# A block-causal attention and two-MoE-layer kernel on one core: weights, x and activations moved to multiples of 2048 or 512 bytes of SBUF, with two buffers of exponentials in place of three

## The chip, the cores and the metric

The kernel runs on one core of one Trainium2 chip. The metric is the device time of one execution in microseconds (us). A core has a matrix engine (TensorE, called PE here, with PEld for its loads of the stationary operand), three engines for elementwise work (VectorE or DVE, ScalarE or ACT, GpSimd or POOL), and SP, which issues the DMAs of this kernel. All of them work on SBUF, 128 partitions wide; an address in this text is the byte offset of a tile inside a partition. PE writes its results to eight banks of PSUM.

## What is computed

Batch 4, 8 heads, 576 positions, head size 64; 2304 tokens of 512 values after attention.

```python
scores = scale * q @ k^T, blocks of 64, causal by block; attn = softmax(scores); x = attn @ v   # x: 2304 x 512
h  = x @ w_in                      # 512 -> 1024
e  = exp(h - max(h)); sm = e / (sum(e) + 1e-09)
solu = h * sm
ln = (solu - mean(solu)) / sqrt(var(solu) + 1e-06) * g_ln
x2 = ln @ w_out                    # 1024 -> 512
h2 = x2 @ w2_in                    # 512 -> 2048
out = (h2 * tanh(softplus(h2))) @ w2_out   # Mish, 2048 -> 512
```

## The kernel before

**Precision.** Nearly every fp32 product is made of three products of fp32r halves: an operand is split into a high part (copied to fp32r) and a low part (the rest), and high x high, high x low and low x high are summed in one PSUM bank. So weights and activations lie in SBUF as pairs: `wih`/`wil`, `woh`/`wol` for the first layer, `w2ih`/`w2il`, `w2oh`/`w2ol` for the second, `xh`/`xl`, `lth`/`ltl`, `x2h`/`x2l`, `gh`/`gl` for what flows through.

**Order of the work.** The program first adds every piece of work to a list (`Plan.add`) with its engine, an estimated cost, the keys that it reads and writes, a priority from the table `PRIO`, and the PSUM banks that it takes and frees. `Plan.order` then walks through time and picks, for each engine, the ready piece of lowest priority number; the instructions are issued in that order, and each engine carries out its own in that order. A piece that writes a buffer waits in this plan for the readers of the buffer's last content, so the number of buffers of a `Rot` (a ring of equal tiles) is one of the things that set the order. Waits on the chip come from the same tiles.

**Stages.**
- Attention, 32 heads (`head`, lines 480 to 722): transposes of k and q, scores, exponentials, normalising on POOL, transposes of the probabilities, the product with v into `xt`. All its tiles lie in the pool `at`.
- First layer, 18 tiles of 128 tokens (`moe1_tile`, line 734), put among the heads as soon as a batch's x is there, the last eight and a half behind the attention. Per tile: x is split into `xh`, `xl` (POOL); line 763 makes h, 24 matmuls of 512 columns into two banks; DVE takes the maxima (776), ACT the exponentials into the tile `e` (781), DVE multiplies with h and normalises in `e` (790), ACT sums squares (795), POOL does the power and the normalising of `e` (801, 803), and line 816 transposes `e` in eight pieces. ACT and DVE split the transposed result into `lth` and `ltl` (823, 824).
- Per two tiles, `moe1_x2` makes x2 (line 833): 96 matmuls of 256 columns, with woh or wol as stationary and lth or ltl as moving operand. x2 goes to DRAM.
- Second layer: six groups of 384 tokens, first with the first 1024 hidden values (half A, weights in the right-hand pool `m2a`, opened when the last head is done), then with the others (half B, weights in the left-hand pool `m2b`, opened when the first layer is done). Per group and chunk of 128 hidden values (`moe2_chunk`): 12 matmuls of 384 columns (line 927), Mish (936), the split into `gh`, `gl`, and 9 matmuls of 512 columns (line 945).

The matmuls that this text speaks of:

```python
 763  nc.tensor.matmul(
 764      out=ps(hp[hf]), lhsT=x.t[:, kk, :], rhs=w[:, kk, hf * 512:(hf + 1) * 512],
 833  nc.tensor.matmul(
 834      out=ps(s)[:, (c % 2) * 256:(c % 2) * 256 + 256], lhsT=w[:, kk, cs], rhs=x.t[:, kk, :],
 927  nc.tensor.matmul(out=h(), lhsT=w[wk][:, kk, ms], rhs=x.t[:, kk, :],
 945  nc.tensor.matmul(out=ps(oslots[t]), lhsT=x.t[:, tsl], rhs=w[wk][:, m, :],
```

`lhsT` is the stationary operand, loaded before each matmul; `rhs` is the moving one. The profile writes `ps<-moving,stationary`.

**Where the tiles lie.** A pool places its tiles one behind the other in the order in which they are made. `const` begins at the bottom; on it stand `m1` (left, first layer) and later, in its place, `m2b`. The right-hand pools (`at`, later `m2a`) are laid so that they end at the top. The table under "The change" has the addresses.

The tiles that the change touches: `e_r`, a ring of three tiles of 4096 bytes (line 727), `g_sb` (line 421, 32 bytes, before the rings of raw weights), `st_r` (line 728, four tiles of 32 bytes), and the ends of `const` and `m2a` (`open_right`, line 870).

Of the kernel before, what the change touches and what calls it, by code (L numbers as in the profile page):

```python
# [10 lines left out]
F32 = mybir.dt.float32  # L11
# [189 lines left out]
def kernel(  # L201
# [17 lines left out]
    P = 128  # L219
    KD = DM // P  # L220
    KF = DFF // P
# [39 lines left out]
    const = ctx.enter_context(tc.tile_pool(name="const", bufs=1))  # L261
# [17 lines left out]
    m1 = m1_cm.__enter__()  # L279
# [138 lines left out]
    wil = m1.tile([P, KD, DFF], F32R, name="wil")  # L418
    woh = m1.tile([P, KF, DM], F32R, name="woh")
    wol = m1.tile([P, KF, DM], F32R, name="wol")  # L420
    g_sb = m1.tile([P, KF], F32, name="g_sb")
    raw1 = Rot(m1, "wraw", 2, (P, 512, 2), I32)
    em1 = Rot(m1, "wem", 2, (P, 2, 512), I32)

# [299 lines left out]

    xh_r = Rot(m1, "xh", 2, (P, KD, P), F32R)
    xl_r = Rot(m1, "xl", 2, (P, KD, P), F32R)
    e_r = Rot(m1, "e", 3, (P, 2, 512), F32)
    st_r = Rot(m1, "st", 4, (P, 8), F32)
    jk_r = Rot(m1, "jk", 1, (P, 2, 512), BF16)
    lth_r = Rot(m1, "lth", 1, (P, KF, 2 * P), F32R)  # L730
    ltl_r = Rot(m1, "ltl", 1, (P, KF, 2 * P), F32R)
    xo_r = Rot(const, "xo", 2, (P, 2, 256), F32)

    def moe1_tile(i, xts, lth, ltl):
        xh, xl = xh_r.next(), xl_r.next()
# [134 lines left out]
    def open_right():  # L870
        at_cm.__exit__(None, None, None)
        cm = tc.tile_pool(name="m2a", bufs=1, side="right")
        p = cm.__enter__()
        opened["r"] = cm
        for nm, shape in (("i", [P, KD, NA * P]), ("o", [P, NA, DM])):
            for x in "hl":
                wa_h[nm + x] = p.tile(shape, F32R, name=f"w2{nm}{x}a")
        x2r_r.make(p)
        x2h_r.make(p, 1)
        x2l_r.make(p, 1)  # L880

    def open_left():
        m1_cm.__exit__(None, None, None)
        cm = tc.tile_pool(name="m2b", bufs=1, side="left")
        p = cm.__enter__()
        opened["l"] = cm
        for nm, shape in (("i", [P, KD, NB * P]), ("o", [P, NB, DM])):
            for x in "hl":
                wb_h[nm + x] = p.tile(shape, F32R, name=f"w2{nm}{x}b")
        x2h_r.make(p)  # L890
        x2l_r.make(p)
        for r in (s_r, gh_r, gl_r, ob_r, raw2, em2, ac_r):
            r.make(p)
# [105 lines left out]
    for b in range(B):  # L999
# [5 lines left out]
        while nt < NTILE and (nt + 1) * P <= (b + 1) * S:  # L1005
# [3 lines left out]
            if nt % 2 == 1:  # L1009
                moe1_x2(nt // 2, *lts[nt // 2])  # L1010
            nt += 1
    o = add(HOST, 0.0, open_right, w=[RIGHT], prio=-1000)
    o.deps.update(heads)
    weights2(0, raw1, em1, WP2A, RIGHT)
# [46 lines left out]
```

## Time and profile before

| | |
|---|---|
| three runs | 875.48, 878.86, 877.20 us; median 877.2 |
| the profiled execution | 877.13 us in all, span of its instructions 875.3 us |
| TensorE clock granted, mean over the span | 0.996 |
| busy share: PE, PEld, DVE, ACT, POOL | 97%, 87%, 58%, 59%, 39% |
| DMA | 74.50 MB, mean 85 GB/s |

A busy PE is not PE at its peak: matmuls overlap, and the ends that the profile gives them are modelled, so the mean duration of one (say 337 ns) is longer than the time from one start to the next. The pace is read from the chain of waits instead, where a piece such as "x24" is so many matmuls of one line back to back and its duration is their time from start to start. The profile's 40 slices are about 22 us each.

### The profile page before, as it was taken

The page shows a single profiled execution, that of the slowest core. Times are in us where ns is not written, and L with a number is a line of the kernel's source. Part 1 is how long each engine was busy: PE and PEld are TensorE (multiplying, and loading weights), DVE is VectorE, ACT ScalarE, POOL GpSimd, SP SyncE. Part 2 cuts the span into 40 slices and gives each one's busy share as a digit, 9 for nine tenths or more (in the row PEclk, how much of TensorE's full clock was granted, in tenths as well). Part 3 has the DMA queues.
Part 4 walks back from the last instruction along what each step waited for, and adds up shares of the span by engine and source line. Part 5 has one row for each costly group of instructions (what it writes and reads, how often), then busy time and mean ns, then how long its engine had stood idle before and what let it go on. Part 6 is the DMA issues. An engine that isn't in the chain of part 4 may idle for free.

```text
span 875.3 us, 14647 instructions
## 1 busy us (share of the span) xinstructions
PE 852.8 (97%) x5152; PEld 764.3 (87%) x5152; DVE 509.4 (58%) x1259; ACT 513.6 (59%) x1278; POOL 339.0 (39%) x440
## 2 busy tenths in 40 slices
PE   4999999999999999999999999999999999999998
PEld 4777878778999999999999899988998989999996
DVE  6889898999887885899962646621111122122121
ACT  6999879888787874666653767643333233133231
POOL 5877867779675551533112334212011011011000
PEclk9999989999999999999999999999999999999999
DMA  8554433413523101523322454321022031230120
GB/s 205 116 135 117 97 100 98 107 37 68 122 47 77 40 14 41 162 101 109 106 69 80 133 180 142 100 72 43 31 73 73 1 109 26 82 109 29 46 73 36
DMA packets 108009, 74.50 MB, mean 85 GB/s; under 512 B 84128, under 2 KB 94880, under 8 KB 107936
## 3 DMA queue, kind: packets, MB, share of 16 engines
q1 hardware_dynamic: 107936, 73.57, 29.2%
q8 instruction: 40, 0.66, 0.3%
q14 instruction: 33, 0.27, 0.1%
HBM read 59.40 MB, written 14.16 MB: 84 GB/s over the span
## 4 chain that ended last, share of the span: by engine, by line
PE 85%; DVE 8%; ACT 5%; DMA 1%; issue 1%; POOL 0%; SPq 0%; ACTq 0%; DVEq 0%
PE ps L927 21%; PE ps L945 21%; PE ps L833 11%; PE ps L763 10%; PE ps L566 5%; PE ps L700 5%; PE ps L648 4%; PE ps L673 3%; PE ps L530 2%; PE ps L816 2%; ACT pt L608 1%; DMA wraw<-in_moe_w_in_dram 1%; DVE nmx L589 1%; DVE ptl L256 1%; PE ps L533 1%
## 5 line engine op out<-in xcount | busy, mean ns | idle before, releaser
L256 DVE TENSOR_TENSOR gl<-s,gh 128x384 fp32r<-128x384 f32 x96 | 61.7, 644 | 247.9 <-ACT gh L250 247.9
L936 ACT ACTIVATE s<-ps 128x384 f32<-128x384 f32 x96 | 47.1, 490 | 193.7 <-PE ps L927 193.5
L259 POOL TENSOR_TENSOR x2l<-x2r,x2h 128x384 fp32r<-128x384 f32 x48 | 52.2, 1116 | 239.9 <-ACT x2h L250 221.4
L608 ACT ACTIVATE pt<-ps,nmx 128x288 f32<-128x288 f32 (+2 forms) x192 | 91.5, 491 | 19.8 <-DVE nmx L589 11.8
L631 POOL TENSOR_SCALAR pt<-pt,sm 128x64 f32<-128x64 f32 (+4 forms) x160 | 86.5, 561 | 39.4 <-DVE sm L626 16.6
L833 PE MATMUL ps<-lth,woh 128*128 128x256 f32 x288 | 82.8, 288 | 0.1
L833 PE MATMUL ps<-lth,wol 128*128 128x256 f32 x288 | 80.8, 281 | 0.0
L833 PE MATMUL ps<-ltl,woh 128*128 128x256 f32 x288 | 80.8, 280 | 0.0
L589 DVE TENSOR_REDUCE nmx<-ps 128x1 f32<-128x448 f32 (+3 forms) x192 | 73.9, 419 | 5.5 <-PE ps L566 3.4
L700 PE MATMUL ps<-identr,pt 128*128 128x128 f32 x480 | 69.5, 280 | 2.0 <-DVE xt L658 0.7
L927 PE MATMUL ps<-x2h,w2ilb 128*128 128x384 f32 x192 | 64.7, 337 | 0.0
L927 PE MATMUL ps<-x2h,w2ihb 128*128 128x384 f32 x192 | 64.7, 337 | 0.0
L927 PE MATMUL ps<-x2l,w2ihb 128*128 128x384 f32 x192 | 64.6, 337 | 0.0
L927 PE MATMUL ps<-x2h,w2iha 128*128 128x384 f32 x192 | 64.6, 336 | 0.0
L927 PE MATMUL ps<-x2h,w2ila 128*128 128x384 f32 x192 | 64.6, 336 | 0.0
L927 PE MATMUL ps<-x2l,w2iha 128*128 128x384 f32 x192 | 64.4, 335 | 0.0
L566 PE MATMUL ps<-kth,qt 128*128 128x288 f32 (+2 forms) x192 | 58.2, 315 | 3.1 <-ACT qt L250 1.7
L700 PEld LDWEIGHTS ps<-identr,pt 128*128 128x128 f32 x480 | 54.0, 143 | 4.9 <-ACT ptw L711 1.0
L945 PE MATMUL ps<-w2oha,gl 128*128 128x512 f32 x144 | 57.1, 396 | 0.2 <-DVE gl L256 0.2
L945 PE MATMUL ps<-w2oha,gh 128*128 128x512 f32 x144 | 56.9, 395 | 0.1
L945 PE MATMUL ps<-w2ola,gh 128*128 128x512 f32 x144 | 56.8, 394 | 0.0
L945 PE MATMUL ps<-w2ohb,gl 128*128 128x512 f32 x144 | 56.2, 391 | 0.0
(126 smaller groups left out, 2411.3 us busy)
## 6 DMA issues: line engine op xcount, KB each, us to landing
wraw<-in_moe_w_in_dram SPq DMA_DIRECT2D x24, 512.0 KB, 4.7
wraw<-in_moe_w_out_dram SPq DMA_DIRECT2D x24, 512.0 KB, 3.7
kraw<-in_k_dram SPq DMA_DIRECT2D x60, 160.0 KB, 3.0
x2r<-x_d SPq DMA_DIRECT2D x12, 768.0 KB, 4.8
qraw<-in_q_dram SPq DMA_DIRECT2D x31, 160.0 KB, 2.6
x_d<-xo SPq DMA_DIRECT2D x18, 256.0 KB, 2.3
acc_d<-ob SPq DMA_DIRECT2D x18, 256.0 KB, 2.2
ac<-acc_d SPq DMA_DIRECT2D x18, 256.0 KB, 5.5
```

The lines of the kernel that those rows point to most:

```text
L256: nc.vector.tensor_tensor(out=dst, in0=src, in1=hi.bitcast(F32), op=ALU.subtract)
L259: nc.gpsimd.tensor_tensor(out=dst, in0=src, in1=hi.bitcast(F32), op=ALU.subtract)
L566: nc.tensor.matmul(out=dst, lhsT=qt.t[:, t * P:(t + 1) * P], rhs=m.t[:, c0:c1], start=(i == 0), stop=(i == 1))
L589: nc.vector.tensor_reduce(out=nmx.t[:, j:j + 1], in_=ps(s)[:, o:o + c1 - c0], axis=AX.X, op=ALU.max, negate=True)
L608: add(ACT, c_act(c1 - c0, acc=True), lambda t=t, o=o, c0=c0, c1=c1, j=j: nc.scalar.activation(out=pts[t].t[:, c0:c1], in_=ps(s)[:, o:o + c ...
L631: nc.gpsimd.tensor_scalar(pp, pp, sm.t[:, t:t + 1], 1.0, op0=ALU.mult, op1=ALU.mult)
L700: nc.tensor.transpose(ps(s)[:, i * P:(i + 1) * P], pts[t].t[:, j * P:(j + 1) * P], ident)
L763: nc.tensor.matmul(out=ps(hp[hf]), lhsT=x.t[:, kk, :], rhs=w[:, kk, hf * 512:(hf + 1) * 512], start=bool(first), stop=bool(last))
L833: nc.tensor.matmul(out=ps(s)[:, (c % 2) * 256:(c % 2) * 256 + 256], lhsT=w[:, kk, cs], rhs=x.t[:, kk, :], start=(kk == 0 and i == 0), stop ...
L927: nc.tensor.matmul(out=h(), lhsT=w[wk][:, kk, ms], rhs=x.t[:, kk, :], start=(kk == 0 and i == 0), stop=(kk == KD - 1 and i == 2))
L936: add(ACT, c_act(G2), lambda: nc.scalar.activation(out=s.t, in_=h(), func=AF.Mish), r=[hk, LEFT], w=[s.key()], rel=[hp], prio=pri("f_v" + ...
L945: nc.tensor.matmul(out=ps(oslots[t]), lhsT=x.t[:, tsl], rhs=w[wk][:, m, :], start=(m == 0 and i == 0), stop=(m == n - 1 and i == 2))
```

## The change

It makes no new instruction and takes none away. It does four things to the tiles:
- the ring of exponentials has two tiles of 4096 bytes, not three;
- `g_sb` and the four `st` tiles, 32 bytes each, are made last in the pool `m1`, behind all its large tiles;
- `const` gets a tile of 320 bytes that nothing uses (`edge_c`), so that the left-hand pools begin at 6144 = 3 x 2048;
- `m2a` gets a tile of 2016 bytes that nothing uses (`edge_r`), so that it begins at 143360 = 70 x 2048.

```diff
-    g_sb = m1.tile([P, KF], F32, name="g_sb")
...
-    e_r = Rot(m1, "e", 3, (P, 2, 512), F32)
-    st_r = Rot(m1, "st", 4, (P, 8), F32)
+    e_r = Rot(m1, "e", 2, (P, 2, 512), F32)
     jk_r = Rot(m1, "jk", 1, (P, 2, 512), BF16)
     lth_r = Rot(m1, "lth", 1, (P, KF, 2 * P), F32R)
     ltl_r = Rot(m1, "ltl", 1, (P, KF, 2 * P), F32R)
     xo_r = Rot(const, "xo", 2, (P, 2, 256), F32)
+    const.tile([P, 80], F32, name="edge_c")
+    g_sb = m1.tile([P, KF], F32, name="g_sb")
+    st_r = Rot(m1, "st", 4, (P, 8), F32)
...
 x2l_r.make(p, 1)
+        p.tile([P, 504], F32, name="edge_r")
```

Addresses of the built programs. Within a tile every matmul operand begins at a whole multiple of 512 bytes from the tile's start, so the remainder by 64 or 512 holds for all of them.

| tiles | used by | before: first address, remainder by 512, by 64 | change: first address, remainder by 512 |
|---|---|---|---|
| wih, wil, woh, wol | 763 moving, 833 stationary | 5824: 192, 0 | 6144: 0 |
| xh, xl | 763 stationary | 106208: 224, 32 | 106496: 0 |
| lth, ltl | 833 moving | 128864: 352, 32 | 124928: 0 |
| w2ih, w2il of half A | 927 stationary | 145376: 480, 32 | 143360: 0 |
| w2oh, w2ol of half A | 945 moving | 178144: 480, 32 | 176128: 0 |
| first x2h, x2l | 927 moving, groups 1, 3, 5 of each half | 217056: 480, 32 | 215040: 0 |
| second x2h, x2l | 927 moving, groups 2, 4, 6 of each half | 71360: 192, 0 | 71680: 0 |
| w2ih, w2il of half B | 927 stationary | 5824: 192, 0 | 6144: 0 |
| w2oh, w2ol of half B | 945 moving | 38592: 192, 0 | 38912: 0 |
| gh, gl | 945 stationary | 91328: 192, 0 | 91648: 0 |
| e | 816 stationary | 114400: 224, 32 | 114688: 0 |
| all tiles of the attention but xt, identr | | unchanged | unchanged |

The shorter ring changes the order that the plan gives. PE's order is the same for its first 900 matmuls and again from the second layer on; in between, the same instructions stand in another sequence. Two places, both on PE.

The first is where the orders part: h of the fourth tile of the first layer (763) and the transposes (816, in the change 817) of the second tile. `ps_..` are PSUM banks, `pth`, `ptl` and `vs` belong to the attention. Before:

```order
L673 MATMUL ps_64<-pth_145,vs_113 128x128
L673 MATMUL ps_64<-ptl_149,vs_113 128x128
L816 MATMUL ps_68<-identr,e_166 128x128 x4
L763 MATMUL ps_67<-wih,xh_162 128x512
L763 MATMUL ps_63<-wih,xh_162 128x512
L763 MATMUL ps_67<-wil,xh_162 128x512
L763 MATMUL ps_63<-wil,xh_162 128x512
L763 MATMUL ps_67<-wih,xl_164 128x512
L763 MATMUL ps_63<-wih,xl_164 128x512
L816 MATMUL ps_64<-identr,e_166 128x128 x4
```

In the change the same eight transposes:

```order
L647 MATMUL ps_63<-ptw_154,vraw_101 64x256 x2
L647 MATMUL ps_63<-ptw_155,vraw_101 64x256
L647 MATMUL ps_63<-ptw_155,vraw_101 64x128
L817 MATMUL ps_66<-identr,e_165 128x128 x4
L817 MATMUL ps_70<-identr,e_165 128x128 x4
L699 MATMUL ps_65<-identr,pt_1_127 128x128
```

Before, the fourth tile's h, of which the last six matmuls are shown, was begun ahead of these transposes, since its exponentials go into another buffer than the second tile's; in the change all of it stands behind them, and attention work has moved up. Counted over the whole order, 36 matmuls of line 763 stand in the change where 63 stood before, in the 69 us of PE's work that follow the first difference.

The second is behind the attention, at the end of a pair of tiles, where x2 of the pair before (833, in the change 834) gives way to the transposes of this pair and then to h of the next pair (763, in the change 764). Before:

```order
L833 MATMUL ps_64<-lth_173,wol 128x256
L816 MATMUL ps_70<-identr,e_167 128x128 x4
L833 MATMUL ps_63<-lth_173,woh 128x256
...
L833 MATMUL ps_63<-lth_173,wol 128x256
L816 MATMUL ps_66<-identr,e_165 128x128 x4
L816 MATMUL ps_65<-identr,e_167 128x128 x4
L816 MATMUL ps_67<-identr,e_165 128x128 x4
L763 MATMUL ps_64<-wih,xh_162 128x512
```

In the change, at the last three of the four pairs that stand behind the attention:

```order
L834 MATMUL ps_69<-lth_167,wol 128x256
L817 MATMUL ps_67<-identr,e_164 128x128 x4
L817 MATMUL ps_65<-identr,e_164 128x128 x4
L817 MATMUL ps_66<-identr,e_165 128x128 x4
L817 MATMUL ps_68<-identr,e_165 128x128 x4
L764 MATMUL ps_63<-wih,xh_160 128x512
```

In both, all sixteen transposes of a pair stand ahead of the next pair's h. Before, four of them were put twelve matmuls of x2 earlier.

## Rows read from the trace of the kernel before

**Rows 1.** The page: busy time of the engines, and the chain by engine.
```profile
span 875.3 us, 14647 instructions
...
PE 852.8 (97%) x5152; PEld 764.3 (87%) x5152; DVE 509.4 (58%) x1259; ACT 513.6 (59%) x1278; POOL 339.0 (39%) x440
...
PE 85%; DVE 8%; ACT 5%; DMA 1%; issue 1%; POOL 0%; SPq 0%; ACTq 0%; DVEq 0%
```
**Rows 2.** Stretches: length, busy PE, PEld, DVE, ACT, POOL (instructions), granted clock, DMA.
```profile
171.00:240.00 69.00, 67.02 (x482) 60.21 (x481) 62.31 (x171) 56.33 (x155) 54.52 (x77) 1.00 0.30 72
240.00:345.00 105.00, 104.71 (x799) 99.31 (x798) 86.44 (x244) 80.22 (x232) 54.78 (x87) 1.00 0.16 40
345.00:400.00 55.00, 55.00 (x352) 49.37 (x351) 44.50 (x98) 31.65 (x64) 19.66 (x22) 1.00 0.42 135
...
660.00:760.00 100.00, 100.00 (x502) 90.64 (x501) 17.97 (x29) 29.79 (x62) 12.76 (x12) 1.00 0.20 64
```
**Rows 3.** Waits of PE from 171 to 345 us: total, times, longest.
```profile
PE ps L700 <- DVE xt L658: 0.7, 1, 0.7
...
PE ps L566 <- DVE ktl L256: 0.2, 1, 0.2
```
**Rows 4.** Chain of waits, second layer: start us, duration us, line, matmuls.
```profile
613.55 4.19 PE ps L927 x24
...
642.88 4.17 PE ps L927 x24
...
661.65 10.48 PE ps L945 x45
672.13 4.24 PE ps L927 x24
676.37 4.08 PE ps L945 x18
...
713.79 4.18 PE ps L927 x24
...
838.56 16.66 PE ps L927 x96
855.23 16.38 PE ps L945 x72
```
**Rows 5.** Chain of waits, first layer behind the attention, one pair of tiles.
```profile
367.22 11.40 PE ps L763 x48
378.62 9.96 PE ps L833 x84
388.58 0.44 PE ps L816 x4
389.02 1.42 PE ps L833 x12
390.44 1.31 PE ps L816 x12
391.75 11.19 PE ps L763 x48
```
**Rows 6.** Groups of PE's instructions by line and form: count, busy us, mean ns.
```profile
L833 PE MATMUL ps<-ltl,woh 128*128 128x256 f32 x288 | 80.8, 280 | 0.0
...
L927 PE MATMUL ps<-x2h,w2ihb 128*128 128x384 f32 x192 | 64.7, 337 | 0.0
...
L945 PE MATMUL ps<-w2oha,gl 128*128 128x512 f32 x144 | 57.1, 396 | 0.2 <-DVE gl L256 0.2
```
**Rows 7.** Line 763 in two stretches: length, busy PE (matmuls), PEld, clock, DMA.
```profile
240.00:345.00 105.00, 25.52 (x96) 16.68 (x95) 1.00 0.16 40
345.00:459.00 114.00, 49.26 (x204) 37.83 (x204) 1.00 0.34 109
```
**Rows 8.** POOL in order of time: normalising of the two tiles e of the pair of rows 5.
```profile
387.79 1.20 POOL L803 TENSOR_SCALAR e<-e,st 128x1024 f32<-128x1024 f32 x1
...
389.62 1.21 POOL L803 TENSOR_SCALAR e<-e,st 128x1024 f32<-128x1024 f32 x1
```

## The prediction

> **What bounds the kernel now.** I read the page first: PE is busy for 97% of the span, no other engine for more than 59%, and 85% of the chain that ended last is PE's [rows 1]. The stretches then say where it is the bound. From 240 us on, PE is busy for all but a few tenths of a microsecond of each stretch, at a granted clock of 1.00 (the 2.4 GHz level), while DVE falls from 81% (44.50 of 55 us) behind the attention to 18% in the second layer [rows 2]. There the time is the number of matmuls times the pace of one, and the chain of waits gives that pace, piece by piece. Only up to about 240 us, with DVE busy for 62.31 of 69 us, do other engines hold PE up [rows 2].
>
> **The pace goes with the addresses.** The matmuls of 512 columns in line 945 took 10.48 / 45 = 232.9 ns each at 661 us, with the weights of half A, and 4.08 / 18 = 226.7 ns fifteen microseconds later with those of half B; at the end 16.38 / 72 = 227.5 ns [rows 4]. Same line, same form, same stationary tiles gh and gl, same clock and equally quiet neighbours [rows 2]. What differs is the moving operand's address: half A's lie 32 bytes past a multiple of 64 and gh and gl do not, half B's lie on one like gh and gl. Line 763, also of 512 columns, pairs a moving operand on a multiple of 64 with a stationary one 32 past it, and takes 11.19 / 48 = 233.1 ns [rows 5]. In line 927, 384 columns, half B with the first x2h (32 past, weights on a multiple) takes 4.24 / 24 = 176.7 ns, with the second x2h (both on a multiple) 4.18 / 24 = 174.2 and 16.66 / 96 = 173.5 ns; half A took 4.19 / 24 = 174.6 ns with the first x2h (both 32 past), 4.17 / 24 = 173.8 with the second (weights 32 past) [rows 4]. So a mismatch by 32 between the two operands costs 5.4 ns at 512 columns, and 2 to 3 at 384 in one of its two kinds.
>
> Where both share a remainder, its value hardly shows: half A with the first x2h has both operands at 480 past a multiple of 512, half B with the second has both at 192, and they take 174.6 and 173.5 to 174.2 ns. The change brings every pair to remainder 0 by 64, 512 and mostly 2048. By these rows it earns what the match by 64 earns, and the larger multiples nothing further.
>
> **The sum, part by part.** Taken against the profiled execution's 877.13 us, which is the median (877.2) to 0.1 us.
> - Line 945, half A: three groups of 144 matmuls [rows 6], 432 x (232.9 - 227.5) = 2.3 us, all on the path.
> - Line 927, half B, the three of six groups with the first x2h: half of three times 192 [rows 6], 288 x (176.7 - 174.1) = 0.7 us, with the mean of the three matched pieces; 0.6 to 0.9 us by the slowest and the fastest of them. For the other 864 at most 0.7 ns, 0.6 us; I take nothing.
> - Line 763: 96 + 204 matmuls lie where PE is the bound [rows 7], 300 x (233.1 - 227.5) = 1.7 us. The other 132 of the 432 lie among attention heads where PE also waits; between nothing and 0.7 us, and I take nothing. The lower end of the whole term is 0: at 384 columns the same kind of pair (second x2h, weights of half A) shows no loss.
> - Line 833, 3 x 288 matmuls of 256 columns [rows 6], is mismatched now (lth 32 past, woh on a multiple) and no row has a matched one. They take 9.96 / 84 = 118.6 ns [rows 5]. In proportion to columns the gain would be 2.7 ns each, 2.3 us; the line through 5.4 at 512 and 2.6 at 384 comes to nothing at 256; and the matched pace of 384 less 128 columns' worth (227.5 - 173.5 = 54 ns) is 119.5, a loss of 0.8 us. I take the middle of the three, 0.5 us.
> - Transposes, scores and products of the attention keep their addresses: nothing. Elementwise work on the moved tiles and the DMAs that land in them may gain or lose a little; behind 240 us PE covers them with DVE at 82% (86.44 of 105 us) or less [rows 2]. The two tiles that nothing uses cost no instruction.
> - The order. In the 69 us behind the first difference 27 matmuls of line 763, 27 x 0.233 = 6.3 us of PE's work, give way to attention work, which leans on DVE; DVE has 69 - 62.3 = 6.7 us free there [rows 2]. If it absorbs this, nothing is lost; if none of it, PE waits for some 4 us more, part of which comes back later, when the line 763 work fills other holes. On the other side, all the waits of PE between 171 and 345 us come to 2.2 us in five lines, from 0.7 to 0.2 us [rows 3]: a better order earns no more than about that. I take 0.
> - Two buffers of e behind the attention. The exponentials of the next pair may start when the transposes of this pair have read e; these stand ahead of the next pair's h in both orders, and the exponentials follow h. No wait is added. What must not be late is e itself: POOL ends the second tile's at 389.62 + 1.21 = 390.83, 12.2 us behind the end of h at 378.62 [rows 5, 8]. In the changed order its transposes start behind 8 x 12 matmuls of line 833 (9.96 + 1.42 = 11.4 us) and eight transposes (0.9 us), at 12.3 us [rows 5]. It just fits, and POOL's ends are rough: before, PE began that tile's transposes at 390.44, less than 0.4 us ahead of the end shown, and did not wait. I take 0.
>
> 2.3 + 0.7 + 1.7 + 0.5 = 5.2 us; 877.1 - 5.2 = **871.9 us**. The low ends are 2.3 + 0.6 + 0 - 0.8 - 4 for the order = -1.9, 879.0 us; the high ones 2.3 + 1.5 + 2.4 + 2.3 + 2.2 = 10.7 us, 866.4.
>
> **Rivals.**
> *The larger multiples count.* Between 384 and 512 columns a matched matmul grows by 54 ns for 128 columns, 0.422 ns a column; 512 columns by themselves are 216 ns, 384 are 162. Some 11.5 ns per matmul are left over at both sizes, and nothing in the rows says that they are not a cost of starting off a multiple of 512 or 2048, since no operand of lines 763 to 945 does so now. If all of it went, line 945 would gain 432 x 16.9 + 432 x 11.5, line 927 some 1152 x 12, line 763 300 x 17.1, line 833 864 x 10: 7.3 + 5.0 + 13.8 + 5.1 + 8.6 = 39.8 us, 837 us; with a third of it about 860. Against it: 480 and 192 past a multiple of 512 differ by a nanosecond at most [rows 4], and a cost of starting badly would hardly be so equal at both. The Trainium skill, TensorE: Matmul & The Clock Gate, Back-to-back issue gap, gives N / 2.4 + 2.5 ns for a single matmul's gap, which at 512 columns is 215.8 ns; no run here shows it with fp32r operands and a new stationary one each time.
>
> *Addresses count for nothing.* The step between halves A and B could come from what else is different, the order of groups or the PSUM banks, and the change would then leave 877 us, give or take the 2 us of the order. For it: the pair of second x2h and half A's weights is mismatched and runs at the matched pace. Against it: at 512 columns both kinds of mismatch lie at 233 ns and the only matched pair at 227. The Trainium skill speaks for this rival: SBUF — State Buffer, Specifications, has lines of 16 bytes and a penalty for each step to a new one, and all addresses of before are multiples of 32, so that by it nothing is left to align. The trace disagrees by the 5.4 ns above.
>
> *Slower: the shorter ring makes PE wait for e.* One mechanism: with all sixteen transposes at the end of the pair's 11.4 us of x2, each microsecond by which the chain of e (maxima, exponentials, product, squares, power, normalising: 12.2 us now) grows is a microsecond of PE, for the slack is 0.1 us by POOL's ends, and each pair of tiles pays it again, as do the tiles among the heads, whose h must now wait for the tile two ahead. To be slower by over 0.5% (4.4 us, about what a measurement of this kernel can tell from no change) it must first eat the 5.2 us: some 10 us in all, or 1.1 us for each of the nine pairs. DVE at 81% behind the attention [rows 2] has work of the next weights that can stand ahead of the chain, and in the trace of before such work already stands in it. Then 882 to 886 us, say 884. Against it: the chain fits by the rows, and faster matmuls do not lengthen it.
>
> **How the numbers follow.** The forecast, matched by 64 and the order neutral within 4 us, has 0.64. Faster means below 872.8; of its range of 866.4 to 879 little more than half lies there, but the terms are less spread than their ends, so I put 0.42 below and 0.22 above. The larger multiples count: 0.08, all faster. Addresses count for nothing: 0.15, the same. Slower: 0.13. So faster 0.50, same 0.37, slower 0.13. The range of 8 in 10 runs from 860, which leaves out most of the first rival, to 881, which leaves out the last.
>
> **What would show it.** In the changed profile, line 945 at 227 to 228 ns from start to start in half A as in half B; line 927 at 173 to 174 in all groups; line 763 at 227 to 228 in the pairs behind the attention; line 833 between 116 and 119.5. PE without idle time from 240 us on, and no wait of line 817 for POOL in the pairs. I am wrong if half A of line 945 stays at 233 (addresses count for nothing), if a 512-column matmul falls below 224 (larger multiples count), or if line 817 shows waits of a microsecond per pair.

## The result, and the profile after

The changed kernel takes 887.15 us (median of four runs, 885.9 to 889.19) against 877.81 us for the kernel before in the same comparison (875.48 to 878.86): a ratio of 1.0112, 95% interval 1.0082 to 1.0143. It is slower by 1.1%, 9 to 10 us, outside the range of 860 to 881 and on the other side of the forecast. Its profiled execution took 886.17 us, with a span of 884.4 us.

Line numbers move by one or two: 763, 816 and 833 are 764, 817 and 834 in the change, 927 and 945 are 929 and 947; of the attention, 566, 673 and 700 are 565, 672 and 699. The page of the change, busy time and the chain by engine, beside [rows 1]:

```profile
span 884.4 us, 14632 instructions
...
PE 855.7 (97%) x5152; PEld 766.6 (87%) x5152; DVE 514.1 (58%) x1259; ACT 512.1 (58%) x1278; POOL 339.8 (38%) x440
...
PE 81%; DVE 10%; ACT 3%; issue 2%; DMA 2%; POOL 2%; SPq 0%; ACTq 0%; DVEq 0%; POOLq 0%
```

The shares hardly tell the two kernels apart. The chain does: PE's part of it fell from 85% to 81%, and DVE's rose. The stretches, to be read beside [rows 2]:

```profile
171.00:240.00 69.00, 64.43 (x473) 57.33 (x472) 61.17 (x164) 56.99 (x164) 54.06 (x78) 1.00 0.33 79
240.00:345.00 105.00, 104.13 (x745) 96.68 (x743) 78.85 (x225) 68.59 (x196) 53.28 (x83) 1.00 0.14 35
345.00:400.00 55.00, 52.45 (x362) 48.70 (x363) 41.15 (x93) 32.41 (x73) 17.07 (x22) 0.97 0.32 106
```

PE lost 2.6 us of busy time in 171 to 240 us and 2.5 us in 345 to 400 us, where it had been the bound. DVE is not busier there than before (61.17 against 62.31 us in the first): it did not become the bound. The pace of the matmuls, in the chain of waits (start, duration, line, matmuls), beside [rows 4, 5]:

```profile
395.33 10.93 PE ps L764 x48
406.26 11.51 PE ps L834 x96
...
670.99 10.24 PE ps L947 x45
681.24 4.18 PE ps L929 x24
685.42 4.12 PE ps L947 x18
...
847.64 16.66 PE ps L929 x96
864.30 16.38 PE ps L947 x72
```

Line 764 runs at 10.93 / 48 = 227.7 ns (233.1 before), line 947 in half A at 10.24 / 45 = 227.6 (232.9), as forecast. Line 834 is slower: 11.51 / 96 = 119.9 ns, 118.6 before. So the paces at 512 columns came as forecast, and the time went somewhere else.

Where it went is seen in the matmuls of h alone. First the kernel before, line 763, then the change, line 764 (length, busy PE and its matmuls, PEld, granted clock, DMA):

```profile
171.00:240.00 69.00, 16.29 (x61) 10.82 (x62) 1.00 0.30 72
...
345.00:364.00 19.00, 8.61 (x36) 6.69 (x36) 1.00 0.42 137
```

```profile
171.00:240.00 69.00, 8.05 (x30) 5.27 (x30) 1.00 0.33 79
240.00:345.00 105.00, 35.28 (x138) 24.81 (x138) 1.00 0.14 35
345.00:364.00 19.00, 0.00 (x0) 0.00 (x0) 0.91 0.05 16
```

Before, 61 matmuls of h stand among the heads between 171 and 240 us; in the change 30. The 31 that are missing are 31 x 0.23 = 7.1 us of work that needed nothing from the heads then in progress. They come later: from 240 to 345 us 138 matmuls of h stand where 96 stood before [rows 7], and the attention is put off by them. It runs to 363.6 us instead of 345.4 us (its last matmul), and in its last 19 us no h stands beside it. What PE waits for in the change from 171 to 560 us (total, times, longest):

```profile
PE ps L672 <- DVE xt L687: 1.6, 1, 1.6
PE ps L699 <- POOL qs L259: 1.0, 1, 1.0
PE ps L565 <- DVE ptl L256: 0.9, 2, 0.6
PE ps L817 <- POOL e L804: 0.9, 1, 0.9
PE ps L565 <- ACT pt L607: 0.8, 1, 0.8
PE ps L672 <- ACT pt L607: 0.7, 1, 0.7
```

With six smaller ones the waits come to 8.3 us, against 2.4 us before in the same stretch. Some 6.2 us of them are attention matmuls that wait for the attention's own steps on DVE, ACT and POOL. One wait of 0.9 us is for `e`.

The longest of these waits ends at 346.3 us, and a lower clock follows it. All engines in the change, before and after 347 us:

```profile
343.00:347.00 4.00, 2.00 (x15) 1.65 (x15) 3.93 (x8) 1.63 (x5) 2.75 (x3) 1.00 0.01 4
347.00:351.00 4.00, 3.68 (x19) 3.00 (x17) 3.97 (x13) 3.63 (x14) 0.00 (x0) 0.57 0.00 0
```

PE was busy for 2.00 of 4 us, and most of the next four went at the lower level of 1.2 GHz (a mean of 0.57). Part of the loss in 345 to 400 us is this clock.

### The profile page after: what moved, and what is told of

Its sections match the earlier page's. It is cut to its first block, busy times and chain, and to the rows that moved or that the text cites. A ratio compares the mean times of both kernels' runs of the same rounds, so it can differ in the third digit from the quotient of the medians.

```text
span 884.4 us, 14632 instructions
## 1 busy us (share of the span) xinstructions
PE 855.7 (97%) x5152; PEld 766.6 (87%) x5152; DVE 514.1 (58%) x1259; ACT 512.1 (58%) x1278; POOL 339.8 (38%) x440
## 4 chain that ended last, share of the span: by engine, by line
PE 81%; DVE 10%; ACT 3%; issue 2%; DMA 2%; POOL 2%; SPq 0%; ACTq 0%; DVEq 0%; POOLq 0%
PE ps L929 21%; PE ps L947 21%; PE ps L834 10%; PE ps L764 9%; PE ps L699 5%; PE ps L565 4%; PE ps L647 4%; PE ps L672 3%; PE ps L817 2%; PE ps L529 2%; DVE nmx L588 2%; DVE ptl L256 1%; DMA wraw<-in_moe_w_in_dram 1%; PE ps L532 1%; ACT pt L607 1%
## 5 line engine op out<-in xcount | busy, mean ns | idle before, releaser
L607 ACT ACTIVATE pt<-ps,nmx 128x288 f32<-128x288 f32 (+3 forms) x192 | 91.6, 492 | 18.5 <-DVE nmx L588 10.1
L947 PE MATMUL ps<-w2olb,gh 128*128 128x512 f32 x144 | 56.5, 392 | 0.0
```

What stands on the lines that cost most here:

```text
L607: add(ACT, c_act(c1 - c0, acc=True), lambda t=t, o=o, c0=c0, c1=c1, j=j: nc.scalar.activation(out=pts[t].t[:, c0:c1], in_=ps(s)[:, o:o + c ...
```

## The experiments

The change mixes two things, an order and addresses. The orders of the instructions can be compared engine by engine with names and buffer numbers left out: the first kernel below has exactly the order of the change, the next two have exactly that of before. So these three, with before and the change, hold the one while the other moves.

**Two buffers of e alone.**

```diff
-    e_r = Rot(m1, "e", 3, (P, 2, 512), F32)
+    e_r = Rot(m1, "e", 2, (P, 2, 512), F32)
```

> The kernel before with two buffers of e instead of three and nothing else; every tile behind e moves down by 4096 bytes, so all remainders modulo 512 and 2048 stay as they were, and the order of the work becomes that of the changed kernel. Theory (the two buffers make a worse order, and the addresses give back some 3 us): slower than before by 10 to 13 us, 888 to 891 us, that is as slow as the changed kernel or up to 3 us slower; matmuls of L763 in the second half of the first layer stay near 233 ns and those of the first half (256 columns, now L833) near 118.6 ns; TensorE stands still some 10 us longer in all between 171 and 460 us. Rival (the new addresses cost, the order costs nothing): 877 us, within 2 us of before.

Measured: 891.79 us (889.74 to 893.26), ratio 1.0158, interval 1.0138 to 1.0179, 12.1 to 15.7 us over before. The theory held, with a little more than the 888 to 891 us that it gave; the rival falls. Its stretches:

```profile
171.00:240.00 69.00, 64.43 (x478) 57.55 (x478) 61.69 (x168) 57.19 (x161) 55.08 (x79) 1.00 0.32 78
...
345.00:400.00 55.00, 51.78 (x366) 47.92 (x365) 41.63 (x92) 32.18 (x74) 21.44 (x28) 0.97 0.28 92
```

PE loses the same 2.6 us in 171 to 240 as in the change, and its order is the change's, at the remainders of before. The order is the loss.

**Addresses alone, common remainders by 64.** Three buffers; `g_sb` and `st` behind the large tiles, and a spare tile of 32 bytes in `m2a`:

```diff
-    g_sb = m1.tile([P, KF], F32, name="g_sb")
...
-    st_r = Rot(m1, "st", 4, (P, 8), F32)
...
     xo_r = Rot(const, "xo", 2, (P, 2, 256), F32)
+    g_sb = m1.tile([P, KF], F32, name="g_sb")
+    st_r = Rot(m1, "st", 4, (P, 8), F32)
...
+        p.tile([P, 8], F32, name="edge_r")
```

> The kernel before with its three buffers of e and its order; only the places of tiles change, so that both operands of nearly all matmuls of the MoE layers start at the same remainder modulo 64 (not at multiples of 512 or 2048). Theory (order costs, common remainders are worth 2.3 + 1.7 + 0.7 us and cost 1.2 us at the 256-column matmuls of L833, where they go from 118.6 to 119.9 ns): 877.5 - 3.5 = 874 us, range 872 to 875.5. Rival (the new addresses cost the 10 us of the changed kernel): 885 to 889 us. A third reading (multiples of 512 or 2048 are needed for the faster pace): 877.5, L945 half A at 232.9 ns as before.

Measured: 875.66 us (874.25 to 878.82), ratio 0.9979, interval 0.9967 to 0.9991: faster by 0.8 to 2.9 us, at the weak end of the theory, whose range ended at 875.5. The rival falls, and so does the third reading: every matmul operand of these lines lies 192 or 448 past a multiple of 512 here, yet the chain shows the paces of the change (lines 927 and 945 are 928 and 946 here):

```profile
461.51 11.51 PE ps L833 x96
...
661.28 10.24 PE ps L946 x45
...
837.92 16.66 PE ps L928 x96
854.59 16.38 PE ps L946 x72
```

To the last digit these are the change's 11.51, 10.24, 16.66 and 16.38 us. Multiples of 512 or 2048 add nothing to a common remainder by 64.

**The same, but lth and ltl 32 bytes off.** `g_sb` now stands ahead of `lth`:

```diff
+    g_sb = m1.tile([P, KF], F32, name="g_sb")
     lth_r = Rot(m1, "lth", 1, (P, KF, 2 * P), F32R)
```

> As the run before it, but the activations that L833 reads (lth, ltl) stay 32 bytes past a multiple of 64, as in the kernel before, while all other operands have common remainders. Theory (a 256-column matmul runs faster when its operands do not start at a common remainder, the longer ones slower): L833 at 118.6 ns instead of 119.9, so 1.2 us less than the run with all remainders common: 872.5 us, range 871 to 874.5, 4 to 5 us under before. Rival (remainders of L833 make no difference, its 1.3 ns in the changed kernel come from the order): the same time as that run, L833 at 119.9 ns in both or 118.6 ns in both.

Measured: 873.92 us (872.65 to 877.05), ratio 0.9968, interval 0.9952 to 0.9983. This overlaps the interval of the run before it, so the pace decides. Line 833 in its chain:

```profile
425.05 9.80 PE ps L833 x84
```

9.80 / 84 = 116.7 ns, against 11.51 / 96 = 119.9 with a common remainder and 118.6 before. At 256 columns the sign of the pairing is the reverse of that at 512. The expected 118.6 ns was too slow: before, lth lay 160 bytes past the weights' remainder by 512, here it lies 32 past it, and the pace is better again by 1.9 ns. What decides there was not tried.

The Trainium skill, SBUF — State Buffer, Specifications (TRN2), knows lines of 16 bytes with a penalty for each step to a new one. All addresses here are multiples of 32, so by that rule alone no shift of this kind could move a pace. The trace disagrees: 32 bytes at lth and ltl are 119.9 against 116.7 ns.

**Two buffers beside the attention only.** Three tiles in memory; the first ten take two of them in turn:

```diff
+    e_at = (0, 1) * 5 + (2, 0, 1, 2, 0, 1, 2, 0)
...
-        e, st = e_r.next(), st_r.next()
+        e, st = Buf(e_r, e_at[i]), st_r.next()
```

> The kernel before at its own addresses, with three buffers of e in memory, of which the first ten tiles (those whose first-layer work lies beside the attention) take only two in turn, and the last eight tiles all three. TensorE's order is that of the kernel with two buffers up to the attention's end, and near to that of before behind it. Theory (the third buffer is worth its time beside the attention, where matmuls of h fill TensorE's waits): 11 to 14 us over before, 888 to 891.5 us, nearly as slow as two buffers throughout (891.8). Rival (each pair of tiles waits behind the attention, as the prediction's slower case had it, 1.1 us a pair): 877 to 882 us, at most the five pairs of the first ten tiles.

Measured: 889.79 us (888.79 to 890.93), ratio 1.0130, interval 1.0113 to 1.0146, about 11.4 us over before. The theory held, and the rival's 877 to 882 us falls.

**Two buffers behind the attention only.** As above with

```diff
+    e_at = (0, 1, 2) * 3 + (0,) + (2, 0) * 4
```

> The kernel before at its own addresses, with three buffers of e for the first ten tiles and two in turn for the last eight, whose work lies behind the attention; TensorE's order up to the attention's end is that of before. Theory (the loss is beside the attention): 0 to 3 us over before, 877 to 880.5 us, with PE busy 67 of 69 us in 171 to 240 as before. Rival (pairs behind the attention wait): 1.1 us for each of four pairs, 881 to 883 us or, if all of the 14 us come from there, 888 to 892.

Measured: 881.84 us (880.04 to 883.29), ratio 1.0034, interval 1.0018 to 1.0050, about 3.0 us over before. As a time this is above the theory's range and inside the rival's; as a difference it is the theory's upper end, under the rival's 4.4 us (four pairs of 1.1). Its stretches, and its waits of PE from 171 to 560 us:

```profile
171.00:240.00 69.00, 66.81 (x480) 59.93 (x479) 62.06 (x169) 56.06 (x156) 54.12 (x76) 1.00 0.30 72
...
345.00:400.00 55.00, 53.40 (x341) 47.64 (x341) 44.17 (x94) 31.51 (x63) 18.10 (x21) 1.00 0.43 136
```

```profile
PE ps L817 <- POOL e L804: 2.8, 3, 1.6
```

Here the rival's mechanism is seen by itself: three waits of the transposes for `e`, 2.8 us in all, for the four pairs behind the attention. Both parts together are 11.4 + 3.0 = 14.4 us, against 13.9 us (1.0158 x 877.38) for two buffers throughout. So some four fifths of the loss come from the ten tiles beside the attention, where h is missing, and one fifth from the eight behind it, where PE waits for e. The division is rough: of the 11.4 us, 1.5 are one wait for e behind the attention.

**Two buffers, the change's addresses, another order.** Eight rows of the table of priorities have other numbers, steps of the first layer only (of these lines the entries that differ):

```diff
-    "m_x": (-615.19, 0.87), "m_v": (-299.69, 0.28), "m_w": (539.81, 0.79), "m_u": (-532.04, 0),
-    "m_t": (-668.03, 4.54), "m_e": (-561.52, 3.08), "m_2": (84.9, 2.27), "m_o": (-1269.73, 1.74),
+    "m_x": (-873.58, 169.74), "m_v": (-152.45, 4.86), "m_w": (309.31, 3.19), "m_u": (-751.58, 47.55),
+    "m_t": (-484.77, 23.16), "m_e": (-211.97, 24.75), "m_2": (-134.48, 0.43), "m_o": (-4068.99, 2.3),
```

> The changed kernel with two buffers of e and its addresses, and other numbers in eight rows of the table of priorities (m_x, m_v, m_w, m_u, m_t, m_e, m_2, m_o: the first MoE layer's steps other than h), so that another order comes out. Theory (what costs is the order that the old numbers give with two buffers, not the second buffer as such): 878 to 883 us, 4 to 9 us under the changed kernel (887.2), with fewer and shorter waits of TensorE in 171 to 240 and 345 to 400 us. Rival (with two buffers the h that fills the attention's gaps cannot be had in any order): 885 to 889 us.

Measured: 880.69 us (876.47 to 885.0), ratio 1.0027, interval 1.0002 to 1.0052. The time is as the theory has it: about three quarters of the loss are back (0.27% over before in place of 1.12%) with the same two buffers, and the rival falls. The place is in part another: it came back behind 240 us, where PE is the bound again, and not in 171 to 240:

```profile
171.00:240.00 69.00, 64.12 (x449) 58.03 (x448) 60.17 (x155) 52.63 (x147) 49.95 (x72) 0.95 0.30 72
```

In that stretch this order has a loss of its own. PE waits once, from 208.8 us on, for the low half of the first layer's second weight, and the clock falls behind it:

```profile
PE ps L834 <- DVE wol L410: 3.3, 1, 3.3
```

```profile
208.00:212.00 4.00, 1.11 (x10) 0.91 (x8) 4.00 (x2) 0.30 (x1) 3.92 (x7) 1.00 0.22 51
212.00:219.00 7.00, 6.61 (x30) 6.31 (x31) 4.92 (x14) 4.17 (x12) 1.05 (x1) 0.53 0.10 24
```

Attention matmuls wait there for 1.6 us, against 4.3 us in the change.

**Another order for all of it, and lth off by 32.** `g_sb` ahead of `lth` as above, and these numbers (the 27 entries that differ):

```diff
+    "q": (3095.21, 18.86), "v": (641.43, 56.65), "tr": (-1768.06, 28.0), "sc": (-2973.93, 15.6), "mx": (807.18, 1.98),
+    "ex": (-2028.32, 68.8), "pe": (-1402.39, 23.05), "pv": (-399.07, 1.8), "po": (446.12, 1.53),
+    "ex_0": (-1250.99, 40.24), "pe_0": (-1948.12, 1.56), "pt_0": (-1250.81, 7.56), "pv_0": (-1552.55, 34.5),
+    "sc_0": (-2541.88, 4.91), "te_0": (344.29, 38.49), "tr_0": (-5435.03, 18.67),
+    "wi": (522.98, 29.38), "w2a": (3736.97, 64.62),
+    "m_h": (-353.11, 0.64), "m_v": (-4681.99, 324.36), "m_w": (3896.02, 139.86), "m_u": (-925.83, 13.14),
+    "m_s": (1018.68, 3.5), "m_l": (1860.95, 1.61), "m_t": (-7456.87, 4.99),
+    "f_xA": (760.97, 376.56), "f_sA": (-710.09, 163.33),
```

> The changed kernel with two buffers of e, with other numbers in 27 rows of the table of priorities (attention, weights and first layer), and with the activations of L833 (lth, ltl) moved 32 bytes past a multiple of 64. Theory (order, and the pace of L833): 874 to 880 us; the matmuls of L833 at 117 to 118 ns instead of 119.9 (worth 1.5 to 2.5 us), those of L945 and L763 as in the changed kernel. Rival (two buffers cost whatever the order): 884 us or more.

Measured: 872.27 us (869.21 to 873.51), ratio 0.9934, interval 0.9917 to 0.9952. With two buffers it beats both kernels, by more than I expected. Line 834 takes 11.21 us for 96, 116.8 ns:

```profile
391.16 11.21 PE ps L834 x96
```

The stretches, with all engines and then for line 764 alone:

```profile
171.00:240.00 69.00, 68.12 (x519) 64.26 (x517) 53.12 (x154) 49.85 (x143) 46.25 (x68) 1.00 0.33 78
...
345.00:400.00 55.00, 55.00 (x383) 50.97 (x382) 41.08 (x103) 32.61 (x75) 22.29 (x30) 1.00 0.29 92
```

```profile
171.00:240.00 69.00, 17.42 (x66) 11.67 (x66) 1.00 0.33 78
...
345.00:364.00 19.00, 11.72 (x48) 8.79 (x48) 1.00 0.23 70
```

66 matmuls of h stand among the heads in 171 to 240, and PE is busy for 68.12 of 69 us. Of x2 180 matmuls stand there too, where before and the change have 96. The attention ends even later than in the change, at 371.1 us, with 48 matmuls of h beside its end, and PE is busy throughout. So a late attention need not cost; in the change nothing of the first layer stands beside it from 345 to 351 us, where x2 begins.

**A third buffer with that table.** The table above, three tiles of e, and no tile `edge_c`; `edge_r` has 32 bytes, so that the addresses are those of the run with lth and ltl 32 bytes off, with the same remainders by 64 as the run above. Against the run above:

```diff
-    e_r = Rot(m1, "e", 2, (P, 2, 512), F32)
+    e_r = Rot(m1, "e", 3, (P, 2, 512), F32)
...
-    const.tile([P, 80], F32, name="edge_c")
...
-        p.tile([P, 504], F32, name="edge_r")
+        p.tile([P, 8], F32, name="edge_r")
```

> Three buffers of e with the table of priorities that was found for two (27 rows other than in the kernel before), at addresses whose remainders modulo 64 are those of the fastest run so far (872.3 us, two buffers, same table). Theory (the numbers of the table give a good order only with the number of buffers they were found for, so that a third buffer can lose time as the second's loss did): slower than that run, 876 to 884 us, with more waiting of TensorE between 171 and 400 us. Rival (a third buffer only gives freedom and can cost nothing): 872 us or less.

Measured: 881.21 us (877.94 to 882.92), ratio 1.0034, interval 1.0021 to 1.0048. With the third buffer this table gives an order that is slower by about 1% (1.0034 against 0.9934, each with the kernel before). Two rows show it, all engines and then line 763 alone:

```profile
171.00:240.00 69.00, 65.13 (x445) 57.71 (x444) 56.42 (x158) 49.27 (x144) 47.88 (x69) 1.00 0.32 74
```

```profile
171.00:240.00 69.00, 23.45 (x90) 15.96 (x90) 1.00 0.32 74
```

PE is busy for 65.13 us where it was for 68.12 with one buffer less. More freedom gave the plan another order, not a better one. It is not short of h: 90 matmuls of line 763 stand in this stretch, 66 with two buffers and 61 in the kernel before. So the number of them alone does not say what PE loses; that their places among the heads decide is my reading, and no run tries it.

**The change with lth off by 32.** The change with `g_sb` ahead of `lth` and nothing else, so that its order stays:

```diff
-    g_sb = m1.tile([P, KF], F32, name="g_sb")
...
+    g_sb = m1.tile([P, KF], F32, name="g_sb")
     lth_r = Rot(m1, "lth", 1, (P, KF, 2 * P), F32R)
```

> The changed kernel with its order and its two buffers; only lth and ltl start 32 bytes later, 32 past a multiple of 64, and so no longer at the remainder of the weights that L833 reads with them. Theory (the common remainder costs the 256-column matmuls): 864 times 2.9 ns, from 119.9 to 117.0 ns, 2.5 us under the changed kernel: 884 to 886 us. Rival (the pace of L833 follows the order of the work): 887 us, L833 at 119.9 ns.

Measured: 886.52 us (884.07 to 887.15), ratio 1.0088, interval 1.0067 to 1.0109. The interval overlaps the change's (1.0082 to 1.0143), and the median lies between the theory's 884 to 886 us and the rival's 887, so the time does not settle it. The chain does. Line 834:

```profile
405.29 11.21 PE ps L834 x96
```

11.21 / 96 = 116.8 ns in the order of the change too, against 11.51 / 96. The pace belongs to the address, not to the order.

**All of them in one count.** For each instruction of PE I took the time from its start to the next one's start, less the lower quartile of this time for the same line and form in the runs compared, and summed what was over 0.1 us, in microseconds by stretch:

| kernel | 0 to 171 | 171 to 240 | 240 to 345 | 345 to 400 | 400 to 560 | all |
|---|---|---|---|---|---|---|
| before | 19.5 | 4.0 | 0.6 | 0.3 | 1.0 | 25.4 |
| the change | 18.0 | 8.7 | 3.4 | 3.2 | 2.2 | 35.5 |
| two buffers alone | 21.6 | 8.8 | 1.9 | 5.7 | 1.8 | 39.8 |
| two beside the attention | 19.6 | 9.1 | 1.1 | 4.3 | 3.7 | 37.8 |
| two behind it | 18.4 | 4.2 | 0.6 | 1.9 | 2.5 | 27.6 |
| two, eight rows changed | 18.4 | 9.1 | 1.0 | 0.0 | 0.6 | 29.1 |
| two, 27 rows changed, lth off | 17.6 | 1.3 | 0.7 | 0.0 | 1.4 | 21.0 |
| three with that table, lth off | 17.9 | 7.0 | 1.1 | 0.0 | 3.3 | 29.3 |

Two buffers alone are 39.8 - 25.4 = 14.4 us over before in this count, and 13.9 us by the ratio of their times. The change is 10.1 us over before in the count; by the medians it is 9.3 us. Up to 171 us PE's order is the same in before, the change and two buffers alone; the first column differs there with the clock (at the lower level for some 7 us behind 120 us in before, for as much there and some 3 us behind 20 us in two buffers alone, for nothing in the change). Behind 171 us the change is 17.5 - 5.9 = 11.6 us over before, and two buffers alone 18.2 - 5.9 = 12.3 us.

## Why the prediction was wrong

**The step that failed: the order, "I take 0", and with it "No wait is added".** The prediction saw that 27 matmuls of line 763 give way in the 69 us behind the first difference, and priced the loss at between 0 and 4 us, 0 if DVE absorbs the attention that moves up. DVE's free time was the wrong measure. DVE is no busier than before (61.17 against 62.31 us), and PE's waits in that stretch are for steps of the heads on ACT, DVE and POOL in turn: each head is a chain of short steps over four engines, and h is what PE does meanwhile. With 31 matmuls of h fewer, PE loses 4.7 us more in that stretch by the count (8.7 - 4.0), just over my bound of 4. And the loss was not given back later, as I had supposed: the attention was behind by then, and 5.7 us more were lost up to 400 us (3.4 + 3.2 against 0.6 + 0.3), part of it at the lower clock that follows the longest wait. That the order costs the time is shown by the run with two buffers alone, which has the change's order at the old remainders; that it costs it through the missing h is argued from these waits, since the number of h alone does not give the loss in every run.

**The misreading behind it.** I wrote that all sixteen transposes of a pair stand ahead of the next pair's h in both orders. In the order of before, h runs one tile ahead of the transposes. Of the 432 matmuls of line 763, 204 lie behind 345 us [rows 7], so 228 ahead of it; 36 more follow at 345.65 us and 48 at 367.22 us [rows 5], which makes 312, thirteen tiles:

```profile
345.65 8.44 PE ps L763 x36
```

The sixteen transposes up to 391.75 us [rows 5] are those of the eleventh and twelfth tile. The exponentials of the thirteenth stand in a third buffer by then. That order cannot be had with two. For the same reason the 12.2 us that I gave the chain of e were wrong: the tile that POOL ends at 390.83 us [rows 8] is the twelfth, whose h ended half way through the piece at 367.22, at about 372.9 us; its chain took some 18 us, and the sum that "just fits" compared two different tiles.

**The slower rival**, with 0.13 and 884 us, had the cause, the shorter ring, and was near in size. Its mechanism, PE waiting for e in every pair, is real where it can be seen by itself, at 0.7 us a pair (2.8 us over four pairs; I had written 1.1), but it is the smaller part, and in the change itself one wait of 0.9 us. The larger part stood in it as half a sentence, on h among the heads that must wait for the tile two ahead, and was priced as a wait for e, not as work missing beside the attention. The Trainium skill, Trainium Kernel Development and Optimization, Best Practices, says that consistent bubbles can mean that SBUF ran out. The runs here agree with one limit: a buffer taken away made the bubbles, 4.7 us in 69, but another order with the same two buffers took them out again, down to 1.3 us.

**The terms of the pace** can be read with the order of before held fixed, by the sums from start to start in the profiled executions of the three kernels with that order.
- Line 945, half A: 2.3 us forecast; 101.3 to 99.7 us, a gain of 1.6, of which line 927 of the same half gave 0.2 back (100.7 to 101.0). It is there in the longer pieces alone. Before, and then with the addresses alone, pieces of 27, 18 and 9:

```profile
544.44 6.30 PE ps L945 x27
...
596.78 4.19 PE ps L945 x18
...
636.62 2.08 PE ps L945 x9
```

```profile
544.82 6.16 PE ps L946 x27
...
596.63 4.12 PE ps L946 x18
...
636.19 2.08 PE ps L946 x9
```

27 gain 0.14 us, 18 half of that, nine nothing. I had taken the pace of a piece of 45 for all.
- Line 927, half B: 0.7 us forecast, 0.6 measured (101.09 to 100.49), but line 945 of the same half gave 0.6 back (98.13 to 98.71). Where line 927 took 4.24 us for 24, the 18 matmuls of line 945 behind it took 4.08; where it took 4.18, they took 4.12. 8.32 or 8.30 us: the time only changed sides at the handover. Both values stood in [rows 4], one behind the other, and I used the 4.24 as a cost and the 4.08 as a matched pace. The true term is nothing.
- Line 763: 1.7 us forecast, 1.1 to 1.6 measured (103.4 to 102.3 and 101.8).
- Line 833: a gain of 0.5 us forecast, with a loss of 0.8 as the bound from the matched 384 columns less 128 columns' worth. That row was the right one: 119.5 ns by it, 119.9 measured, a loss of 1.2 us of pace (1.9 with a wait of 0.7 us that this run had). I took the middle of three estimates where the nearest row was at the end.
- Together 1.7 us (0.8 to 2.9) by the run with the addresses alone, where the sum had 5.2.

**The other two rivals** fall. The larger multiples give nothing over a common remainder by 64, and no piece of 512-column matmuls came below 224 ns each. Addresses do not count for nothing: 233 to 228 ns at 512 columns, 119.9 to 116.8 at 256, and a time lower by 0.2% to 0.3% with the order held fixed.

**The sum, closed:** 1.0158 for the order times 0.9979 for the addresses is 1.0137, inside the change's interval of 1.0082 to 1.0143. Why the centre lies lower is not settled. Behind 171 us the two kernels differ by 0.7 us in the count (12.3 against 11.6); the larger difference, 3.6 us, lies ahead of it, where their orders are the same and their clocks are not.

## What to carry to other kernels

When a list of priorities sets the order, a buffer less is another order, not a wait at one place: compare which tiles are alive at once, and look at the independent work that stood in the bound engine's gaps, before calling the shorter ring free. Its amount alone is not the measure (90 matmuls of h beside the heads, and 7.0 us lost; 66, and 1.3). A table tuned for one number of buffers is not tuned for another, in either direction (two buffers 872 us, three with the same table 881 us): search again after each change of a ring. Read a pace over a whole cycle of alternating lines, since one line can gain at a handover what its neighbour loses.

## What the runs showed that I had not expected

*Thirty-two bytes work in both directions.* A common remainder by 64 makes 512 columns faster (233 to 228 ns) and 256 columns slower (118.6 to 119.9 ns); with 32 bytes between the operands and the moving one at another place, 256 columns took 116.7 ns. Which property of the addresses decides is open.

*The granted clock differs between executions of one kernel.* Two kernels whose order is the same up to 171 us, before and the change, 120 to 130 us (busy PE, PEld, DVE, ACT and POOL, granted clock, DMA):

```profile
120.00:130.00 10.00, 9.35 (x43) 7.40 (x43) 8.14 (x30) 6.30 (x19) 7.01 (x10) 0.66 0.26 68
```

```profile
120.00:130.00 10.00, 9.23 (x54) 6.76 (x55) 9.81 (x32) 8.25 (x26) 8.27 (x12) 1.00 0.33 93
```

Of this stretch before, about two thirds went at the lower level of 1.2 GHz (a mean of 0.66), in the change nothing, although PE had been as busy in the ten microseconds ahead of it: 8.75 us before and 8.83 us in the change, both at 1.00. Over its executions the kernel before took 875.9 to 877.1 us where the mean clock was 1.000 in the comparison with the first three runs, 876.9 to 878.8 at 0.996 and 879.2 to 880.1 at 0.994 (in later comparisons three executions at 1.000 took 879.1 to 880.4 too, so the clock is not all of it). Executions with a few microseconds at the lower level were thus mostly some 1 to 3 us longer, as much as the addresses are worth, and kernels are best compared over several executions each.
